# Gated linear attention and an MLP on one core: the gates' row-to-column transfers issued from ScalarE's queue

## The chip, the cores and the metric

The kernel runs on one core of a Trainium2 chip. The metric is the device time of one execution in microseconds (us). A core has five engines that run their own instruction streams: TensorE (PE), VectorE (DVE), ScalarE (ACT), GpSimd (POOL) and SyncE (SP). Transfers between the main memory and the on-chip memory are issued from the instruction stream of an engine; in this kernel all but two are issued from SP. Each stream is in order: an instruction that waits holds up everything behind it on its engine.

## The reference

The four attention inputs are float32. The weights of the MLP come as float64 and are rounded to float32 in the kernel.

```python
# q, k, v, alpha: (B, H, S, D) = (4, 8, 768, 48); alpha in 0.8 .. 1.0
for t in range(S):
    state = alpha[:, :, t, :, None] * state + einsum('bhd,bhe->bhde', k[:, :, t], v[:, :, t])
    y[:, :, t] = einsum('bhd,bhde->bhe', q[:, :, t], state)
x = y.transpose(0, 2, 1, 3).reshape(B, S, H * D)          # (4, 768, 384)
xn = (x - mean(x)) / sqrt(var(x) + 1e-6) * g_ln
out = x + maximum(xn @ w_ch1, 0) @ w_ch2                  # 384 -> 1536 -> 384
```

## The kernel before

The sequence of 768 steps is cut into 6 chunks of 128 rows, and with 4 batches this makes 24 attentions, called `a` to `x` (chunk `n // 4`, batch `n % 4`). Each handles all 8 heads of one batch and one chunk, as 4 pairs. In the chunks after the first, a chunk is treated as two halves of 64 rows.

One attention goes through these steps. ACT takes the logarithm of alpha (`la`, line 278); PE sums it along the rows with a triangular matrix (`lps`, 288); ACT takes the exponential of the sum and of its negative (`eq` and `lps`, 291 and 292); DVE multiplies k and q with them (`qk`, 294 and 296). The last row of `eq` in each half is the *gate*, by which the state is multiplied at the half's end. It lies along a row of one partition, and is wanted as a column, one value for each partition. This is done by two small transfers through main memory: SP writes the row to a buffer `row` (line 301), and later it reads it back as columns of 4-byte elements into `gate` (line 361). In between, PE transposes q and k (`tps`, 321), ACT (in the first chunk also DVE) copies them (`qT`, `kT`, 326 and 328), PE multiplies them (`aps`, 345; 337 in the first chunk) and DVE takes the part below the diagonal into `at` (350, 355). After the gate's transfer PE makes the halves' contributions to the state (`ups`, 371); DVE adds them to the old state and POOL multiplies with the gate (lines 384 and 386; in the first chunk one DVE instruction, 380). The result after the first half is `mid`, after the second the next state `st`. PE makes the output (`yps`, 407; 397 in the first chunk), which reads `mid`. Then come the norm on ACT (414 to 440; the first chunk's line 436 is on DVE), a copy of x to main memory (`kept`, 426), a transpose on PE (`xps`, 446) and a scaled copy (`xT`, 449 or 453).

The MLP of chunk 0 is plain (lines 476 and 488). For the other chunks both products are made with schemes of fewer block products (FIRST with 15 and SECOND with 20), whose sums are made on DVE, ACT and POOL (lines 575, 598 to 604, 739, 765 and on). The weights (`ws`, 192) are rounded in the first 95 us.

The order of all this is written out in the string ORDER: each letter is a turn of one generator (lower case: one attention; `M`, `V`, `N`, `X`, `R`, `S`, `W`, `O`, `Y`, `Z`, `P`, `Q`: parts of the MLP; `A` to `L`: one piece of the weights), which runs to its next `yield` and issues the instructions of one step. So ORDER fixes the order of the instructions on every engine. The waits are put in by the framework. The buffers `row` and `gate` exist four times each. All transfers, whichever engine issues them, take one of eight semaphores in turn, and a transfer waits until the one eight before it has landed.

The gate's step is a turn of its own, with nothing else in it, so that its place among the instructions of any engine can be read from ORDER.

Of the kernel before, what the change touches and what calls it, by code (L numbers as in the profile page):

```python
# [49 lines left out]
def kernel(  # L50
# [36 lines left out]
    nc = tc.nc  # L87
# [6 lines left out]
    NP = H // 2  # L94
# [18 lines left out]
    r = np.arange(P)  # L113
# [151 lines left out]
    def attention(c, b):  # L265
# [32 lines left out]
        ne = 1 if whole else 2  # L298
        row = dram.tile([2, 2 * 64 * NP], FP32, name="row", tag="row")
        gate = work.tile([P, 2, NP], FP32, name="gate", tag="gate", bufs=B)  # L300
# [57 lines left out]
                mask=mask_of_halves.unsqueeze(1).broadcast_to([P, 2 * NP, HS]))  # L358
        yield
        with nc.allow_non_contiguous_dma(reason="two rows to columns"):  # L360
            nc.sync.dma_start(gate[:, :ne], row[:ne].rearrange("o (p r) -> r o p", p=NP))
        yield
        vn, vx = raws["v", c, b]
        heads = [slice(0, 64), slice(64, R)]
# [475 lines left out]
    turns = {"YZ"[h]: first_of_chunk_0(h) for h in range(2)}  # L840
    turns |= {"PQ"[h]: second_of_chunk_0(h) for h in range(2)}
    turns |= {chr(ord("a") + n): attention(n // B, n % B) for n in range(NCB * B)}
    turns |= {chr(ord("A") + i): take_weights(i) for i in range(len(pieces))}
    turns |= {"M": mlp(), "V": hidden_products(NCB - 1), "S": combine_first(), "W": combine_weights(), "R": relus(),
# [34 lines left out]
```

## Time and profile before

| | |
|---|---|
| time, median of 3 runs | 445.36 us (441.68 to 449.35) |
| time of the profiled execution | 447.59 us |
| its span, first to last instruction | 445.8 us |
| mean granted TensorE clock | 0.988 |
| PE busy | 430.2 us (97%) |
| PE weight load busy | 385.2 us (86%) |
| DVE busy | 336.4 us (75%) |
| ACT busy | 202.2 us (45%) |
| POOL busy | 149.1 us (33%) |
| transfers | 45.53 MB in 54973 packets, 26204 of them under 512 B |
| issues of line 361 (gate) | 24, all from SP, between 12.6 and 279.0 us |

The busy time of an engine does not count the issuing of transfers and the waiting for semaphores. In the profile's lines an engine's name with a q (SPq, ACTq) means its instruction stream in such a step. The profiled execution is one execution, and its own time is above the median of the runs.

### The profile page before, as it was taken

The page shows a single profiled execution, that of the slowest core. Times are in us where ns is not written, and L with a number is a line of the kernel's source. Part 1 is how long each engine was busy: PE and PEld are TensorE (multiplying, and loading weights), DVE is VectorE, ACT ScalarE, POOL GpSimd, SP SyncE. Part 2 cuts the span into 40 slices and gives each one's busy share as a digit, 9 for nine tenths or more (in the row PEclk, how much of TensorE's full clock was granted, in tenths as well). Part 3 has the DMA queues.
Part 4 walks back from the last instruction along what each step waited for, and adds up shares of the span by engine and source line. Part 5 has one row for each costly group of instructions (what it writes and reads, how often), then busy time and mean ns, then how long its engine had stood idle before and what let it go on. Part 6 is the DMA issues. An engine that isn't in the chain of part 4 may idle for free.

```text
span 445.8 us, 11607 instructions
## 1 busy us (share of the span) xinstructions
PE 430.2 (97%) x4760; PEld 385.2 (86%) x4760; DVE 336.4 (75%) x654; ACT 202.2 (45%) x499; POOL 149.1 (33%) x164
## 2 busy tenths in 40 slices
PE   7987999999999999999999999997999999999996
PEld 5876988865778889998889998887999899999996
DVE  3895899989898788857679748665587689847873
ACT  6674746742422755653656156263223962014200
POOL 1021021200106472133763241680024680646523
PEclk9997999999999999999999999999899999999999
DMA  8889577782041425424341025200023000010201
GB/s 272 268 239 307 174 208 252 227 283 61 30 92 18 127 73 165 107 73 156 95 90 42 31 74 126 53 1 4 1 90 124 1 1 2 0 52 20 71 19 54
DMA packets 54973, 45.53 MB, mean 102 GB/s; under 512 B 26204, under 2 KB 51036, under 8 KB 54920
## 3 DMA queue, kind: packets, MB, share of 16 engines
q1 hardware_dynamic: 54376, 44.63, 34.2%
q8 instruction: 37, 0.61, 0.6%
q10 hardware_dynamic: 544, 0.17, 0.2%
q14 instruction: 16, 0.13, 0.1%
HBM read 35.25 MB, written 9.53 MB: 100 GB/s over the span
## 4 chain that ended last, share of the span: by engine, by line
PE 84%; DMA 5%; DVE 4%; issue 3%; SPq 2%; POOL 1%; ACT 1%; POOLq 0%; DVEq 0%
PE hps L765 29%; PE ops L588 25%; PE hps L476 7%; PE ops L488 7%; PE yps L407 4%; PE aps L345 3%; PE tps L321 3%; PE ups L371 2%; DMA ra<-in_alpha_dram 2%; PE xps L446 2%; DMA vn<-in_v_dram 2%; PE lps L288 1%; DMA ws<-in_moe_w_ch_dram 1%; POOL ob L604 1%; DMA ob<-kept 1%
## 5 line engine op out<-in xcount | busy, mean ns | idle before, releaser
L604 POOL TENSOR_TENSOR ob<-ob,u 128x192 f32<-128x192 f32 x40 | 25.2, 640 | 79.7 <-DVE ob L601 59.8
L765 PE MATMUL hps<-sum,w 128*128 128x256 f32 x192 | 47.3, 379 | 0.0
L588 PE MATMUL ops<-w,hT 128*128 128x192 f32 x224 | 41.0, 333 | 0.0
L765 PEld LDWEIGHTS hps<-sum,w 128*128 128x128 f32 x192 | 36.2, 190 | 4.8
L588 PEld LDWEIGHTS ops<-w,hT 128*128 128x128 f32 x224 | 38.2, 196 | 0.4
L816 ACT ACTIVATE hT<-hT 128x512 f32<-128x512 f32 x48 | 27.8, 626 | 19.2 <-POOL hT L787 11.9
L765 PE MATMUL hps<-xT,w 128*128 128x256 f32 x136 | 34.7, 380 | 0.0
L476 PE MATMUL hps<-xT,w 128*128 128x256 f32 x144 | 34.2, 391 | 0.1
L488 PE MATMUL ops<-w,hT 128*128 128x384 f32 x96 | 31.8, 486 | 0.0
L386 POOL TENSOR_TENSOR st<-st,gate 112x192 f32<-112x192 f32 x16 | 11.5, 726 | 60.4 <-DVE st L384 60.4
L476 PEld LDWEIGHTS hps<-xT,w 128*128 128x128 f32 x144 | 27.8, 198 | 4.3 <-issue 0.3
L386 POOL TENSOR_TENSOR mid<-mid,gate 112x192 f32<-112x192 f32 x20 | 12.3, 617 | 50.8 <-DVE mid L384 28.8
L598 DVE TENSOR_TENSOR ob<-ops,ob 128x192 f32<-128x192 f32 x50 | 17.1, 352 | 15.7 <-POOL ob L604 8.1
L588 PE MATMUL ops<-ws,sum 128*128 128x192 f32 x160 | 28.6, 326 | 0.0
L765 PEld LDWEIGHTS hps<-xT,w 128*128 128x128 f32 x136 | 25.4, 190 | 3.2
L488 PEld LDWEIGHTS ops<-w,hT 128*128 128x128 f32 x96 | 18.0, 190 | 11.5 <-issue 0.2
L588 PEld LDWEIGHTS ops<-ws,sum 128*128 128x128 f32 x160 | 26.4, 190 | 0.2
L407 PE MATMUL yps<-mid,qT 48*64 48x48 f32 x320 | 23.1, 224 | 3.0 <-issue 3.0
L321 PE MATMUL tps<-consts,qk 128*112 128x128 f32 x176 | 24.2, 275 | 1.2 <-DVE qk L296 1.1
L407 PE MATMUL yps<-vn,at 64*64 64x48 f32 x320 | 22.0, 225 | 1.8 <-issue 1.8
L407 PE MATMUL yps<-st,qT 48*64 48x48 f32 x320 | 23.7, 224 | 0.0
L345 PE MATMUL aps<-qT,kT 48*64 48x64 f32 x640 | 23.7, 222 | 0.0
(230 smaller groups left out, 1170.6 us busy)
## 6 DMA issues: line engine op xcount, KB each, us to landing
ws<-in_moe_w_ch_dram SPq DMA_DIRECT2D x12, 768.0 KB
vn<-in_v_dram SPq DMA_DIRECT2D x12, 384.0 KB
kept<-x SPq DMA_DIRECT2D x24, 192.0 KB
ob<-kept SPq DMA_DIRECT2D x24, 192.0 KB
out_dram<-ob SPq DMA_DIRECT2D x19, 192.0 KB
ra<-in_alpha_dram SPq DMA_DIRECT2D x16, 192.0 KB
rk<-in_k_dram SPq DMA_DIRECT2D x6, 384.0 KB
rq<-in_q_dram SPq DMA_DIRECT2D x6, 384.0 KB
```

The costliest lines, as they stand in the source:

```text
L321: nc.tensor.transpose(tps[:, p], qk_of(c, b)[:, i, p].rearrange("p a b -> p (a b)")[:, :R], ident)
L345: nc.tensor.matmul(aps[0][halves[1 - i], p, s], kT[rs, p, s], qT[rs, p, s], start=True, stop=True)
L371: nc.tensor.matmul(up[h, p], qk_of(c, b)[ts, 1, p, i, :h.stop - h.start], vn[ts, i, p], start=True, stop=True)
L386: nc.gpsimd.tensor_mul(new, new, by)
L407: nc.tensor.matmul(yps[r][halves[s], i, p], of, by, start=True, stop=True)
L476: nc.tensor.matmul(hps, w1[:, j // 2, f, j % 2 * P:][:, :P], xT_of[0][:, f, bs], start=(f == 0), stop=(f == NF - 1))
L488: nc.tensor.matmul(ops_of[b], hT_of[c][:, j, b], w2[:, j], start=(j == 0), stop=(j == NJ - 1))
L588: nc.tensor.matmul(acc, lhs[:, j], rhs[:, j], start=(j == 0), stop=(j == NT - 1))
L598: nc.vector.tensor_add(x, acc, x)
L604: getattr(nc.gpsimd, f"tensor_{op}")(x, x, y)
L765: nc.tensor.matmul(acc[:, i], w, b, start=True, stop=True)
L816: nc.scalar.activation(out=x, in_=x, func=AFT.Relu)
```

## The change

One line differs: the gate's second transfer, from `row` back into columns, is issued from ScalarE's instruction stream in place of SyncE's. ORDER stays as it is, so the issue stands between the ACT instructions of the turns around it. The first transfer, of the row to main memory, stays on SP, as do all others.

```diff
@@ -358,7 +358,7 @@
                 mask=mask_of_halves.unsqueeze(1).broadcast_to([P, 2 * NP, HS]))
         yield
         with nc.allow_non_contiguous_dma(reason="two rows to columns"):
-            nc.sync.dma_start(gate[:, :ne], row[:ne].rearrange("o (p r) -> r o p", p=NP))
+            nc.scalar.dma_start(gate[:, :ne], row[:ne].rearrange("o (p r) -> r o p", p=NP))
         yield
         vn, vx = raws["v", c, b]
         heads = [slice(0, 64), slice(64, R)]
```

## The prediction

> **What bounds the kernel now.** I read the page from the top: busy shares, the chain that ended last, then who waited for whom, then the two queues that the change touches.
>
> ```profile
> PE 430.2 (97%) x4760; PEld 385.2 (86%) x4760; DVE 336.4 (75%) x654; ACT 202.2 (45%) x499; POOL 149.1 (33%) x164
> ...
> PE 84%; DMA 5%; DVE 4%; issue 3%; SPq 2%; POOL 1%; ACT 1%; POOLq 0%; DVEq 0%
> ```
>
> TensorE is busy for 430.2 of 445.8 us and is 84% of the chain; ScalarE is 45% busy and 1% of the chain, SyncE's queue 2%. A change that touches only ACT and SP can win at most the 15.6 us in which PE is idle, and loses only what reaches PE. Where PE's idle time lies is told by its own waits:
>
> ```profile
> PE yps L407 <- issue: 4.8, 4, 1.8
> PE ups L371 <- issue: 2.3, 1, 2.3
> PE lps L284 <- ACT la L278: 1.4, 1, 1.4
> PE tps L321 <- DVE qk L296: 1.1, 3, 0.5
> ```
>
> The large ones (7.1 us) have no releaser that the profile shows; none names a gate. The tile view of the gate gives the price of what is moved, and who waits for it:
>
> ```profile
> L361 SPq DMA_DIRECT2D gate<-row x24: 355/392/733, 12.6 to 279.0; - x24
> ...
>   DMA gate<-row: 7.5, 2
> ```
>
> Twenty-four issues of 392 ns (median) on SP; only POOL waits for their landing, twice, 7.5 us together (gates f and h). SP itself waited little for the rows before it could issue them:
>
> ```profile
> SPq L361 <- DMA row<-eq: 2.0, 2, 1.2
> ```
>
> **Part 1: what leaves SP.** 24 x 0.392 = 9.4 us of issue, plus 2.0 us of waiting for rows, 11.4 us in all. The queue is seldom what ends a wait. The biggest ACT wait for a load (7.8 us, before the `la` of attention o at 110.75 us) stands behind an SP load that waits for VectorE, with no gate in between. The one place where gates stand before something early is 12.64 to 13.64 us, gates a and b ahead of row d and the weights' transfer at 14.04; these would come about 1 us sooner. VectorE takes those weights only at 21.23 us, in its own order, and was not idle for them. I take 0; the bound is a gain of 1 us there, and of 2 us more in the first 62 us, where the DMA engines are 79 to 87% busy and the 10 gates free 10 x 0.39 = 3.9 us of the queue (half of it, since SP waits for ACT, VectorE or PE between bursts).
>
> **Part 2: what ACT must do.** At its place in the order of turns ACT now issues the transfer. The nearest price is ACT's own two issues at the start:
>
> ```profile
> 0.76 0.38 ACTq L163 DMA_DIRECT2D consts<-consts  x1
> 1.17 0.52 ACTq L176 DMA_DIRECT2D small<-in_moe_g_ln_dram  x1
> ```
>
> The second has elements of 4 bytes too; the mean is 0.45 us, and 24 x 0.45 = 10.8 us, which takes ACT from 202 to 213 us. New waits on ACT: the row's landing, the gate buffer's last reader (four attentions back), and the transfer eight issues back, with which it shares its semaphore. I set the time at which ACT reaches each gate's place (end of the ACT instruction of the turn before) beside SP's issue: a 12.6 to 14.8, d 21.7 to 24.7, f 29.7 to 32.9, l 78.4 to 84.3, k 96.0 to 101.7, p 152.4 to 156.6, t 227.4 to 231.9, x 275.8 to 298.0, w 279.0 to 306.0; the others move by -1.1 (j) to +4 us. Except for j and h, about 1 us earlier, ACT comes no earlier than SP did, so what SP had waited for is there: I take 0 for waiting. For j and h the rows landed at 42 and 43 us, far ahead. The reverse wait (an SP transfer eight issues later, or a row four later, needs the gate landed) is also met: after gates x and w SP's eighth issue is at 327 and 332 us, while they land by 301 and 309.
>
> So the cost is 0.45 us in front of whatever ACT does next. At c, i, m, n, o, p, q, v and w ACT then idles 0.7 to 2.8 us anyway, waiting for PE as a rule: 9 gates hidden. At a and b (0.9 us together, before the qT copy at 14.72) the copy is used 5.7 us after it ends, and the `la` behind it 1.6 us after: hidden. For e, f, g, j, h, l, k, r, t, s, u and x I compared the ends of the next `la`, qT/kT and xn with PE's first matmul that takes them: 0.5 to 20 us of slack, hidden if no two delays add up. Gate d is not covered:
>
> ```profile
> 24.71 0.19 ACT L429 ACTIVATE few<-few 128x1 f32<-128x1 f32 x1
> ...
> 26.00 0.20 ACT L433 ACTIVATE few<-few 128x1 f32<-128x1 f32 x1
> ...
> 25.75 1.75 DVE L436 TENSOR_SCALAR xn<-x,few 128x384 f32<-128x384 f32 x2
> ```
>
> The second L436 starts at 26.23 us, as L433 ends, and is on the chain. I take **+0.45 us** for d. Uncovered, all 24 would cost 10.8.
>
> **Part 3: when the gate lands.** An idle-time SP gate lands 2.4 to 3.1 us after its issue (x: 275.78 to 278.13, by its semaphore); f, behind three loads of 384 KB, took 7.3. On ACT's queue the nearest row is `small`: its last 4-byte packet started at 4.36 us, 3.2 after the issue, while SP's load of 2.11 us needed until 7.35. So a separate queue passes loads that were issued earlier, and I take 3.2 us in the busy first 62 us and 2.6 later. The users:
>
> - a: 14.8 + 3.2 = 18.0, VectorE's `st` moves from 17.20 to 18.0 and ends at 18.35. Below, VectorE idles 0.93 us until 18.49: 0. With 4.0 us (SP's own a) it ends at 19.15: +0.7.
> - f: 32.9 + 3.2 = 36.1, 1 us before POOL got it (37.10). PE's next `yps` stalls until 40.86 for a reason the profile doesn't name: 0 either way, since even 7.3 us gives 40.2 + 0.5 = 40.7.
> - r: 195.5 + 2.6 = 198.1, against 199.06: VectorE's wait of 2.4 us behind it shrinks by up to 1 us; at 4.1 us of latency it grows by 0.6. I take 0; PE has four products of 1.3 us queued there.
> - w: 306.0 + 2.6 = 308.6 against POOL at 307.51: 1.1 late. Its `yps` is the third of three from 306.50 on and needs `mid` near 309.0; POOL now ends at 309.1: **+0.1 us**, with 3.2 us of latency +0.7. Behind it PE has a stall of 1.74 us (310.03) that could take it up.
>
> ```profile
> 17.20 0.35 DVE L380 TENSOR_TENSOR st<-ups,gate 112x192 f32<-112x192 f32 x1
> 18.49 0.55 DVE L294 TENSOR_TENSOR qk<-rk,lps 128x384 f32<-128x384 f32 x1 [0.93 <-ACT lps L292]
> ...
> 307.51 0.51 POOL L386 TENSOR_TENSOR mid<-mid,gate 112x192 f32<-112x192 f32 x1 [3.62 <-DVE mid L384]
> ```
>
> The others are used 2 us or more after they land, except l (84.3 + 3.2 = 87.5, POOL takes it at 88.35; with the 5.2 us it took on SP, 1.1 late).
>
> The row of `small` meets a rule that speaks against a gain: the Trainium skill, page "DMA: Bandwidth & Descriptors", section "Issuing engines are not separate DMA queues", says that transfers run on the same 16 engines whichever engine issues them and that another issuer saves only issue time. By the rule alone gate f would still need 7.3 us and gate a 4.0 us, the sum would be 1.3 us instead of 0.6; `small` speaks for a faster pass, and no run here shows it for a gate yet.
>
> **Sum.** 0.45 (d) + 0.1 (w) = +0.55 us on the profiled execution, 447.59 us (445.8 span, 1.8 around it): 448.1. That execution lies 2.2 us above the median of the runs (445.36), so the prediction is 445.36 + 0.55, rounded to **446.0 us**. Own range: -3 (part 1) to +0.45 + 0.7 + 0.6 + 0.7 + 1.1 = +3.6 us, 442.4 to 449.0, and the runs of before scatter by 4 us on each side.
>
> **Rivals.**
>
> 1. *ACT's issue reaches PE* (slower). The order of turns was laid out with no issue on ACT; if slack of 0.5 us is used up by an earlier delay, each gate costs PE its 0.45 us: 445.4 + 10.8 = 456.2. For: attentions e to v have `la`, qT/kT or xn with slack as small as 0.05 to 0.8 us (t's `la` 0.05, v's and x's xn 0.6). Against: none of these stands right behind a gate, and ACT idles often. It passes 2% when 20 of the 24 are exposed.
> 2. *SP's queue was holding the start* (faster). The 3 us of part 1 plus POOL's 2 us at f and h: 440.4. For: DMA 87% busy at the start. Against: PE waits there for ACT, VectorE or nothing named, not for a load. Even so it stays under 2%; to pass it, 8.9 of PE's 15.6 idle us must go.
> 3. *The gate doesn't land sooner on the other queue*, as the sixteen engines are shared: late landings at a, l, r, w cost 0.7 + 1.1 + 0.6 + 0.7 = 3.1, and d 0.45: 448.9, within 2%.
>
> Apart from these, PE's granted clock was 0.5 in three stretches of 3.4 us (about 1.7 us each); one more or less of them in a shifted start moves the time without any of my steps.
>
> **How the numbers follow.** The forecast (hidden but for half a microsecond) gets 0.55, rival 1 0.23, rival 2 0.10, rival 3 0.12. Two per cent, 8.9 us, is about what a measurement of this kernel can tell from no change. Slower by more: nearly all of rival 1 and a little of rival 3, 0.24. Faster by more: the best end of rival 2 with a clock stretch less, 0.06. Range: 441.0 (rival 2 nearly reached) to 456.0 (nearly all of rival 1); the forecast's own is 442.4 to 449.0.
>
> **What would show it.** Right: ACT busy unchanged but 24 ACTq issues of about 0.45 us, PE's waits still without a named ACT releaser, POOL's wait for gate f shorter than 4.3 us, gate w late by about 1 us. Wrong: ACT issues well above 0.5 us, waits of ACT on row or gate buffers, PE idle over 20 us with `kT`, `qT`, `xn` or `eq` as releasers; or PE idle under 8 us.

## The result: 1.0 % slower, and the profile after

| | before | after |
|---|---|---|
| median of 4 runs each | 444.17 us (441.68 to 449.35) | 449.08 us (448.63 to 451.27) |
| ratio of the times, 95% interval | | 1.0104 [1.0058, 1.0150] |
| profiled execution, its span | 447.59 us, 445.8 us | 448.63 us, 446.8 us |
| mean granted clock in it | 0.988 | 0.991 |
| PE's gaps between its first and last instruction, summed | 10.6 us | 12.4 us |

The change costs 4.9 us by the medians. That is within the 2 per cent that the prediction called no change, and yet the interval leaves no doubt of the sign. The forecast had +0.55 us. A ratio with an interval, here and below, leaves out the runs that took over 1.5% longer than the fastest run of their kernel on their chip; medians, means and the table of the clock take every run. The two profiled executions differ by 1.0 us only, because the one of before lay high for its kernel (447.59 against a median of 444.17), so one pair of traces can't hold the whole answer. That is why the same kernels ran again in the experiments below.

The page of the changed kernel, its busy shares, its two hardware queues and its chain:

```profile
PE 429.1 (96%) x4760; PEld 383.4 (86%) x4760; DVE 336.5 (75%) x654; ACT 202.5 (45%) x499; POOL 149.5 (33%) x164
...
q1 hardware_dynamic: 31464, 44.54, 31.1%
q10 hardware_dynamic: 23456, 0.26, 3.0%
...
PE 85%; DMA 6%; DVE 3%; issue 2%; SPq 1%; POOL 1%; ACT 1%; POOLq 0%; DVEq 0%
```

The work of each engine is the same to 2 us. Some 22,900 packets, nearly all of 4 bytes, have gone from SP's queue (q1) to ACT's (q10), which had 544 packets before. DMA has 6% of the chain in place of 5%.

The tile view of the gate (the same view as before the change: duration of one issue in ns, then first and last issue, who waited for its landing, and the time from issue to landing):

```profile
L361 ACTq DMA_DIRECT2D gate<-row x24: 366/367/465, 14.9 to 307.8; - x24
...
  POOL mid L386: 20.3, 4
  DVE st L380: 1.8, 1
...
DMA to landing us min/median/max: 2.5/2.5/4.4
```

An issue on ACT takes 367 ns, a little under the 0.45 us of the prediction. But POOL, which had waited twice for a gate, 7.5 us together, now waits four times, 20.3 us, and VectorE once, which it had not done. The last row has a trap. "DMA to landing" goes by few transfers here; the single landings, read from the releases in the timeline and the chain, run up to 9.2 us.

The waits of PE, POOL and SP (line waited at, releaser: us in total, times, longest):

```profile
PE yps L407 <- issue: 4.3, 3, 1.8
PE ups L371 <- issue: 2.3, 1, 2.3
...
PE ops L588 <- DVE st L384: 0.4, 1, 0.4
PE yps L407 <- POOL mid L386: 0.4, 1, 0.4
```

```profile
SPq L128 <- DMA gate<-row: 4.1, 1, 4.1
```

The two rows without a named releaser are there as before (6.6 us against 7.1), and three more such rows are new, 2.1 us together (`hps` L476 1.1, `hps` L765 0.7, `yps` L397 0.3). New are also two short waits whose releasers, `st` of VectorE and `mid` of POOL, stand just behind a gate (the one for `mid` is in the control below too, without the change), and three waits of SP for gates that ACT issued: the one shown and two at line 301, 3.2 us together.

The chain, in order of time (start, us, what), shows the two gates that are on it:

```profile
32.99 6.77 DMA gate<-row
...
196.65 4.26 DMA gate<-row
```

Gate f took 6.8 us from its issue at 32.99 us; gate r took 4.3 us in the quiet middle.

**Where the time went, along the span.** I matched the instructions of PE in the two traces one by one and took the difference of their starts, after less before. It is 0.57 us already at 12 us, before the first moved transfer, which is scatter. Then it steps to 1.04 us at 22 us (behind gate a) and 1.47 us at 30 us (a stall of 0.28 us with no named releaser is part of it). Around f, from 36 to 46 us, it runs between 1.1 and 2.3 us, and it is 1.58 us from 50 to 60 us, so that f leaves only 0.1 us in this pair. It is 2.56 us after 61 us (a stall of 1.12 us with no named releaser) and back at 1.44 us at 90 us. It stays at 1.59 us from 100 to 200 us, where seven gates are issued (r is the last). Gate r adds 0.40 us at 202 us, the `hps` stall behind it 0.3 us, gate w 0.1 us at 309 us. From 312 to 316 us the difference falls from 2.38 to 0.75 us. This last step is no gain of the change, as the windows of both traces show (from:to, length, busy time with the number of instructions of PE, of PE's weight load, of DVE, ACT and POOL, then PE's granted clock, the share of the DMA engines and GB/s). First before:

```profile
308.60:312.00 3.40, 1.66 (x111) 1.53 (x101) 3.07 (x6) 2.04 (x6) 0.00 (x0) 1.00 0.02 5
312.00:315.40 3.40, 3.40 (x22) 3.31 (x15) 0.00 (x0) 0.87 (x2) 0.00 (x0) 0.50 0.02 5
```

and after:

```profile
309.50:312.90 3.40, 2.10 (x129) 1.95 (x127) 1.82 (x5) 2.12 (x6) 0.51 (x1) 1.00 0.05 7
312.90:316.30 3.40, 2.17 (x25) 2.11 (x26) 1.46 (x3) 1.05 (x3) 0.00 (x0) 1.00 0.02 5
```

Before, PE had a stretch of 3.4 us at half clock here, which cost it some 1.7 us, half of its length; after had none. So in this pair after was lucky by 1.7 us, and its real cost is larger than the 1.0 us between the profiles.

### The profile page after: what moved, and what is told of

Its sections match the earlier page's. It is cut to its first block, busy times and chain, and to the rows that moved or that the text cites. A ratio compares the mean times of both kernels' runs of the same rounds, so it can differ in the third digit from the quotient of the medians.

```text
span 446.8 us, 11604 instructions
## 1 busy us (share of the span) xinstructions
PE 429.1 (96%) x4760; PEld 383.4 (86%) x4760; DVE 336.5 (75%) x654; ACT 202.5 (45%) x499; POOL 149.5 (33%) x164
## 4 chain that ended last, share of the span: by engine, by line
PE 85%; DMA 6%; DVE 3%; issue 2%; SPq 1%; POOL 1%; ACT 1%; POOLq 0%; DVEq 0%
PE hps L765 29%; PE ops L588 26%; PE ops L488 7%; PE hps L476 7%; PE yps L407 4%; PE tps L321 4%; PE aps L345 3%; DMA gate<-row 2%; PE ups L371 2%; DMA ra<-in_alpha_dram 2%; PE xps L446 2%; DMA rq<-in_q_dram 1%; PE lps L288 1%; DVE at L350 1%; POOL ob L604 1%
## 5 line engine op out<-in xcount | busy, mean ns | idle before, releaser
L765 PE MATMUL hps<-sum,w 128*128 128x256 f32 x192 | 47.3, 379 | 0.0
L765 PEld LDWEIGHTS hps<-sum,w 128*128 128x128 f32 x192 | 36.2, 190 | 4.8
L588 PE MATMUL ops<-w,hT 128*128 128x192 f32 x224 | 39.9, 327 | 0.0
L588 PEld LDWEIGHTS ops<-w,hT 128*128 128x128 f32 x224 | 36.8, 190 | 0.5
L765 PE MATMUL hps<-xT,w 128*128 128x256 f32 x136 | 34.7, 380 | 0.0
L476 PE MATMUL hps<-xT,w 128*128 128x256 f32 x144 | 33.6, 386 | 1.1 <-issue 1.1
L476 PEld LDWEIGHTS hps<-xT,w 128*128 128x128 f32 x144 | 27.4, 195 | 5.1 <-issue 1.3
L765 PEld LDWEIGHTS hps<-xT,w 128*128 128x128 f32 x136 | 25.4, 190 | 3.2
L488 PEld LDWEIGHTS ops<-w,hT 128*128 128x128 f32 x96 | 17.9, 190 | 11.7 <-DVE w L214 0.5
L407 PE MATMUL yps<-vx,at 64*64 64x48 f32 x320 | 22.2, 224 | 2.5 <-issue 2.5
```

Of the source, the lines that this page charges most:

```text
L407: nc.tensor.matmul(yps[r][halves[s], i, p], of, by, start=True, stop=True)
L476: nc.tensor.matmul(hps, w1[:, j // 2, f, j % 2 * P:][:, :P], xT_of[0][:, f, bs], start=(f == 0), stop=(f == NF - 1))
L488: nc.tensor.matmul(ops_of[b], hT_of[c][:, j, b], w2[:, j], start=(j == 0), stop=(j == NJ - 1))
L588: nc.tensor.matmul(acc, lhs[:, j], rhs[:, j], start=(j == 0), stop=(j == NT - 1))
L765: nc.tensor.matmul(acc[:, i], w, b, start=True, stop=True)
```

## The experiments

Two theories stood at the start. **Theory 1, late landings:** a gate on ACT's queue is issued later and lands no sooner, and where its user has little slack (a, f, g, r, w) the delay reaches PE. **Theory 2, ACT's issue:** each of the 24 issues delays ACT's next instruction, and part of that reaches PE. Letters are attentions in order, so that the kernels choose the engine by the letter. Each ratio is that of the kernel's runs to the runs of the kernel before on the same chip.

### Before and after once more

The kernel before, unchanged:

> The kernel before, unchanged, timed against itself. All theories expect 444 us and a ratio of 1.000; its profile shows how far two profiles of one program lie apart. In the profile of after PE's instructions run 0.57 us late from 8 us on, before the first moved transfer is issued at 14.9 us: if that is scatter, this profile scatters as much, and the half-clock stretches (three of 3.4 us before, two after) vary too.

Measured: 444.73 us, ratio 1.0027 [0.9989, 1.0065]. The method tells about 0.4% apart. One of PE's waits in its trace matters below:

```profile
PE yps L407 <- POOL mid L386: 0.3, 1, 0.3
```

This is the wait behind gate f, here with f on SP, and a stall of 1.9 us without a releaser stands behind it, as in the changed kernel.

After, again:

```diff
-            nc.sync.dma_start(gate[:, :ne], row[:ne].rearrange("o (p r) -> r o p", p=NP))
+            nc.scalar.dma_start(gate[:, :ne], row[:ne].rearrange("o (p r) -> r o p", p=NP))
```

> The changed kernel again, on the same chip as the three others. All theories expect 449 us and a ratio of 1.006 to 1.015; a ratio below 1.005 would say that most of the 4.6 us was the chip's scatter, and that the 1.8 us by which PE's instructions are late in the profile are the loss.

Measured: 449.08 us, ratio 1.0129 [1.0081, 1.0177]. The loss is real.

### Five gates moved, and the nineteen others

```diff
+            eng = nc.scalar if "abcdefghijklmnopqrstuvwx"[c * B + b] in "afgrw" else nc.sync
+            eng.dma_start(gate[:, :ne], row[:ne].rearrange("o (p r) -> r o p", p=NP))
```

> Only gates a, f, g, r and w are issued by ACT, the other 19 stay on SP. Theory 1: all of the loss, in the profile PE 1.8 us late at 310 us against the profile of before, by a 0.6, f and g 0.4, r 0.7, w 0.1; about 446 to 448 us. Theory 2: 5/24 of the loss, 445.0 us. Theory 3: f and g alone, SP again held about 4 us by gate g, 445 to 446 us.

Measured: 447.89 us, ratio 1.0107 [1.0061, 1.0153]. Five of the 24 gates cost about as much as all. In its trace PE is 1.2 us later from a on and waits 0.7 us behind r; f landed 6.2 us after its issue, and PE did not wait for it.

```diff
+            eng = nc.sync if "abcdefghijklmnopqrstuvwx"[c * B + b] in "afgrw" else nc.scalar
+            eng.dma_start(gate[:, :ne], row[:ne].rearrange("o (p r) -> r o p", p=NP))
```

> Gates a, f, g, r and w, whose readers waited for the landing in the profile of after, stay on SP; the other 19 are issued by ACT. Theory 1 (the loss is late landing): 0 to 0.5 us over before, about 444.5 us, ratio 1.000. Theory 2 (each issue of 0.37 us on ACT reaches PE): 19/24 of the loss of 4.6 us, 447.8 us, ratio 1.008. Theory 3 (4-byte packets on a queue of their own disturb the loads, and SP waits for gates that have not landed): i and the later ones do this too, but not where loads are dense; 445 us.

Measured: 447.06 us, ratio 1.0071 [1.0031, 1.0110]. This is more than theory 1 allows. The two halves add up to 1.78%, against 1.04 and 1.29% for the whole; measured against the control, which stands at 1.0027 itself, it is 1.24 against 1.02%, and that is no difference within the method's 0.4%. In its trace, PE's distance to the control is 3.0 us at 100 us, 3.4 us at 300 us and 3.1 us at the end, although twelve gates are issued from ACT after 84 us; so nearly all that it lost, it lost early. Of this, 0.9 us stand before the first moved gate (15.3 us), and the largest step, 1.9 us, stands at a stall of 4.3 us without a releaser, up to 43.3 us. The nineteen were then taken in two parts.

### The nineteen in two parts

```diff
+            eng = nc.scalar if "abcdefghijklmnopqrstuvwx"[c * B + b] in "lkmnopqtsuvx" else nc.sync
+            eng.dma_start(gate[:, :ne], row[:ne].rearrange("o (p r) -> r o p", p=NP))
```

> Only gates k to x without r and w (k, l, m, n, o, p, q, s, t, u, v, x; twelve, all issued after 84 us) are issued by ACT. Theory 1 (late landing): none of these has a reader that waited, so ratio 1.000, and PE's instructions keep their distance to the control from 100 us on to within 0.4 us. Theory 2 (each issue on ACT costs PE its 0.37 us): 12 x 0.37 = 4.4 us, ratio 1.010.

Measured: 445.03 us, ratio 1.0016 [0.9979, 1.0052].

Twelve issues of 366 ns on ACT, from 81 to 295 us, cost nothing that this ratio can tell. Theory 2 falls in its full size: at full exposure these twelve would have cost 12 x 0.37 = 4.4 us, 1.0%, and the interval ends at 0.5%. That the issues delay nothing on ACT is shown by its timeline, under part 2 below.

```diff
+            eng = nc.scalar if "abcdefghijklmnopqrstuvwx"[c * B + b] in "bcdejhi" else nc.sync
+            eng.dma_start(gate[:, :ne], row[:ne].rearrange("o (p r) -> r o p", p=NP))
```

> Only gates b, c, d, e, h, i and j, all issued in the first 60 us, are issued by ACT. Theory 1: i can land late (5.6 us in the profile of after), the others are not waited for: ratio 1.000 to 1.003. Theory 2: 7 x 0.37 = 2.6 us, ratio 1.006. Rival of dense loads (any 4-byte packets on their own queue in this stretch cost, read or not): ratio 1.004 to 1.008.

Measured: 446.05 us, ratio 1.0037 [0.9995, 1.0079]. This decides nothing. If the early seven cost something, it is under 0.8%.

### Which of the five

```diff
+            eng = nc.scalar if "abcdefghijklmnopqrstuvwx"[c * B + b] in "fg" else nc.sync
+            eng.dma_start(gate[:, :ne], row[:ne].rearrange("o (p r) -> r o p", p=NP))
```

> Only gates f and g are issued by ACT. Theory 1 (late landing is the loss, with a and r as its places): f and g land late but in a stretch where PE waits anyway, so 0 to 0.5 us; with the time lost to half clock taken out, about 441.8 us against 441.6 before. Rival (the 4-byte packets on a queue of their own among dense loads are the loss: f took 5.9 us and g 9.2 us to land, and SP stood 4 us behind g): the whole 2.7 us of the five gates, 444.3 us. The profile should show the packets of f and g spread over 4 to 5.5 us on the ACT queue.

Measured: 447.20 us, ratio 1.0051 [1.0021, 1.0082], more than I expected. POOL and PE in its trace (the bracket gives the idle time before and its releaser):

```profile
41.06 0.51 POOL L387 TENSOR_TENSOR mid<-mid,gate 112x192 f32<-112x192 f32 x1 [8.90 <-DMA gate<-row]
```

```profile
PE yps L408 <- POOL mid L387: 2.5, 1, 2.5
```

Gate f, issued at 30.98 us, landed 9.9 us later, and PE waited 2.5 us for the `mid` made of it. In the second run of after this wait was 2.1 us, in the first 0.4 us, and with five gates moved there was none. It is not a loss of its own, though: where the wait is long, the stall without a releaser that stands at this place in the other traces is missing. Both together are 1.4 to 2.5 us in the four traces with f on ACT, and 1.6 to 4.3 us in the six with f at its place on SP (1.8 before, 2.2 in the control). So no trace shows what f and g cost, and the 0.5% stands without a cause.

```diff
+            eng = nc.scalar if "abcdefghijklmnopqrstuvwx"[c * B + b] in "ar" else nc.sync
+            eng.dma_start(gate[:, :ne], row[:ne].rearrange("o (p r) -> r o p", p=NP))
```

> Only gates a and r are issued by ACT. Theory 1: PE's instructions are late by 0.5 to 1.3 us from 20 us on (a, through VectorE's st) and by another 0.5 to 0.7 us from 201 us on (r, PE waits for VectorE's st); with half clock taken out 443 to 443.5 us against 441.6. Rival (dense loads, f and g): 441.6 us.

Measured: 446.01 us, ratio 1.0000 [0.9962, 1.0037]. VectorE in its trace:

```profile
19.44 0.36 DVE L381 TENSOR_TENSOR st<-ups,gate 112x192 f32<-112x192 f32 x1 [2.27 <-DMA gate<-row]
```

Gate a landed 5.45 us after its issue and VectorE waited 2.3 us for it; behind gate r PE waited 0.6 us for `st`. Matched to the control, PE is about 1 us later from a on and 0.6 to 0.9 us from r on. The time does not show these 1.6 us; its interval allows 0.37%, which is as much. So for a and r there is a wait in every trace where they were moved, and no loss that this ratio confirms. By the means of all twelve runs and of all 35 of the kernel before, the ratio is 1.0028, and with the clock taken out (below) the two cost 2.0 us (+-0.9).

### Issued earlier, on either queue

If lateness is the fault, a gate issued earlier should not lose, on whichever queue. In the chunks after the first the transfer can stand behind the qT copy of the same attention, some turns earlier. Gates a to d keep their place and SP.

```diff
+                if not whole:
+                    with nc.allow_non_contiguous_dma(reason="two rows to columns"):
+                        nc.scalar.dma_start(gate, row.rearrange("o (p r) -> r o p", p=NP))
...
-        with nc.allow_non_contiguous_dma(reason="two rows to columns"):
-            nc.sync.dma_start(gate[:, :ne], row[:ne].rearrange("o (p r) -> r o p", p=NP))
+        if whole:
+            with nc.allow_non_contiguous_dma(reason="two rows to columns"):
+                nc.sync.dma_start(gate[:, :ne], row[:ne].rearrange("o (p r) -> r o p", p=NP))
```

> Gates a to d stay on SP; the other 20 are issued by ACT, but earlier, right after the qT copy of the same attention (r about 8 us earlier than in the changed kernel). Theory 1: no loss, ratio 0.995 to 1.003; POOL's mid of r and w no longer wait for a landing. Theory 2 (each issue on ACT costs): 20/24 of the loss as before, ratio 1.008. Rival of dense loads: f and g still travel among loads, ratio 1.004 to 1.006.

Measured: 447.24 us, ratio 1.0029 [0.9999, 1.0058]. By this ratio it loses less than after does (the intervals of this and of the second run of after don't meet), but it is not shown to lose nothing: by the means of all runs it is 1.0069, against 1.0102 for the second run of after. It scatters most of all (443.69 to 453.87 us), and its mean clock, 0.990 over 12 runs, is as low as after's. In its trace a new wait stands on ACT, which issues the gate behind the copy and so waits for the row:

```profile
50.45 0.59 ACT L328 COPY qT<-tps 112x512 f32<-112x512 f32 x1 [3.99 <-DMA row<-eq]
```

PE then waited 3.9 us for the `la` behind it (53.2 us), and two half-clock stretches followed (52.7 to 59.5 us). So this version has a loss that late landings don't explain, and it is no clean test of theory 1.

The same place, on SP:

```diff
+                        nc.sync.dma_start(gate, row.rearrange("o (p r) -> r o p", p=NP))
```

> As the last one, but the early issue is on SP, so ACT is as before. Theory 1: not slower than before, ratio 0.990 to 1.000, since r's 2.4 us wait on VectorE in the kernel before goes; theory 2 the same. If SP, which now waits for rows that have just been sent, holds back its loads, up to 1.01.

Measured: 442.90 us, ratio 0.9948 [0.9913, 0.9983], the only version that beats both kernels. Once more:

> The kernel with the early issue on SP once more, to see whether its gain holds: ratio 0.990 to 0.999, about 442.5 us, with less time at half clock than the kernel before (1.6 us against 2.8).

Measured: 442.78 us, ratio 0.9977 [0.9939, 1.0016], an interval that holds 1. Together, 24 runs have a median of 442.8 us, against 444.8 us for the 98 runs of the kernel before: a gain of about 0.4%, shown by the first run and not by the second alone. By the table below, the gain goes with the clock. VectorE and PE in its first trace:

```profile
195.27 0.36 DVE L388 TENSOR_TENSOR st<-ups,mid 112x192 f32<-112x192 f32 x1 [0.62 <-POOL mid L390]
```

```profile
PE yps L411 <- POOL mid L390: 1.6, 1, 1.6
```

At gate r, VectorE's wait is 0.62 us (2.36 us before, 2.76 us after), and POOL has no wait for a gate in this trace (in the second one, a single wait of 3.6 us). PE's gaps add up to 7.0 us, against 10.6 before and 12.4 after.

### The clock, over all runs

Each run has a granted clock. Of the 98 runs of the kernel before, the 9 with a clock of 0.998 or more have a median of 441.1 us, the 37 around 0.996 have 443.5, the 43 around 0.991 have 445.9, and the 9 below 0.9895 have 447.6. A straight line through all runs of all kernels, with one height for each kernel, gives 1.10 us (+-0.14) of time for each microsecond of clock lost, where the loss is (1 - clock) x 445 us. Its heights and losses split the difference:

| | runs | mean, us | clock lost, us | time less 1.10 x loss |
|---|---|---|---|---|
| before | 98 | 444.7 | 2.9 | 441.5 +-0.5 |
| after | 10 | 449.2 | 4.5 | 444.2 +-1.1 |
| five moved | 6 | 447.9 | 3.4 | 444.2 +-1.3 |
| nineteen moved | 12 | 446.7 | 3.5 | 442.8 +-1.0 |
| f, g moved | 12 | 447.1 | 4.2 | 442.5 +-1.0 |
| a, r moved | 12 | 446.0 | 2.2 | 443.6 +-0.9 |
| twelve late moved | 12 | 445.5 | 2.6 | 442.6 +-0.9 |
| seven early moved | 12 | 445.6 | 3.2 | 442.1 +-0.9 |
| earlier, on ACT | 12 | 447.8 | 4.5 | 442.9 +-1.0 |
| earlier, on SP | 24 | 443.0 | 1.3 | 441.2 and 441.9 |

Of after's 4.5 us, 1.10 x 1.6 = 1.8 us go with the clock and 2.7 us (+-1.0) do not. The same 2.7 us (+-1.2) come from the five gates alone, in its parts 2.0 us from a and r and 1.0 us from f and g (+-0.9 each). The twelve late gates stand 1.1 us (+-0.9) above before, which their ratio did not show. The gain of the early issue on SP is all clock: its losses are 1.6 us smaller, and its height is that of before. A straight line shows that the two go together, and not which causes which; the windows below show the order in time.

## Why the prediction was right and wrong

**The forecast and its sum.** The direction, the class and the middle of the span were right: PE's distance is flat from 100 to 200 us, the sum is small, and 449.08 lies just above the forecast's own range (442.4 to 449.0). The sum itself, +0.55 us, was too small by a factor of 8 to 9, and of its two terms the large one, +0.45 us for gate d, measured nothing (part 2). The class was in part luck: rival 3 has the same class with other steps, and it is nearer to what happened.

**Part 1 (SP's queue).** Taken at 0. The traces show no gain there. That SP could gain by *order* was not seen: issued earlier on SP, the gates won 0.4%.

**Part 2 (ACT's issue).** Right that it costs next to nothing, wrong in its price and in one statement. An issue is 367 ns, not 450; ACT is busy for the same 202 us; no wait of ACT for a row or a buffer appeared; the twelve late gates cost 0.16% with zero well inside. But the price does not stand "in front of whatever ACT does next". Gate d, first before and then after:

```profile
23.91 0.49 ACT L291 ACTIVATE more<-lps 128x384 f32<-128x384 f32 x1 [1.06 <-PE lps L288]
```

```profile
24.95 0.49 ACT L291 ACTIVATE more<-lps 128x384 f32<-128x384 f32 x1 [1.25 <-PE lps L288]
25.02 0.37 ACTq L361 DMA_DIRECT2D gate<-row  x1
...
25.75 0.19 ACT L429 ACTIVATE few<-few 128x1 f32<-128x1 f32 x1
```

The issue (25.02 to 25.39 us) runs while L291 is still busy. From L291 to L429 it is 0.80 us, and it was 0.80 us before (23.91 to 24.71): the term of +0.45 us measured 0.00. For 21 of the 24 gates the time between the ACT instructions on both sides of the issue is not more than 0.08 us longer than before. Only a and b, issued one behind the other, put off the qT copy by 0.6 us, and l its next instruction by 0.2 us. The rows from which the price was taken show the same: both issues (0.76 to 1.69 us) lie inside ACT's table load (0.73 to 2.01 us).

The statement that failed is "the reverse wait is also met". It was worked out for the end, behind gates x and w, and not for g:

```profile
41.50 0.37 SPq L128 DMA_DIRECT2D rk<-in_k_dram  x1
46.06 0.37 SPq L128 DMA_DIRECT2D rq<-in_q_dram  x1
```

These are two of SP's issues in the changed kernel, one after the other. SP reached the second at 41.9 us and stood for 4.1 us, since gate g, issued by ACT eight transfers earlier, had not landed until 45.99 us. This `rq` went out 4.7 us later than in the trace of before (41.37 us). PE's distance does not grow between 46 and 60 us, so no price of this shows.

**Part 3 (when the gate lands) is the step that failed**, and in it the number 3.2 us. It came from `small`, which went out when four loads of SP were just starting. The landings that were then measured:

| gate | on SP, before | forecast on ACT | on ACT, measured | effect on PE |
|---|---|---|---|---|
| a | 4.0 us | 3.2, effect 0 | 4.6 to 5.5 | +0.5 to +1.3 us |
| f | 7.3 | 3.2, "0 either way" | 6.2 to 9.9 | none beyond the scatter |
| g | 5.4 | 3.2, 0 | 4.4 to 9.2 | with f |
| r | 4.0 | 2.6, 0 | 4.3 to 4.5 | +0.4 to +0.7 us |
| w | 2.5 | 2.6, +0.1 | 2.4 | +0.1 us |

In the quiet stretches the estimate was right (x 2.15 us, w 2.4 us). Under loads a gate on ACT's queue takes about as long as one on SP's, at times longer, and g was shorter in two of four traces (4.4 and 4.6 us). The timelines of the changed kernel show a and f, with ACT's issue and the user behind it:

```profile
14.86 0.52 ACT L278 ACTIVATE la<-ra 128x384 f32<-128x384 f32 x1 [2.46 <-DMA ra<-in_alpha_dram]
14.93 0.93 ACTq L361 DMA_DIRECT2D gate<-row  x2
```

```profile
19.64 0.36 DVE L380 TENSOR_TENSOR st<-ups,gate 112x192 f32<-112x192 f32 x1 [1.79 <-DMA gate<-row]
19.92 0.54 DVE L294 TENSOR_TENSOR qk<-rk,lps 128x384 f32<-128x384 f32 x1
```

```profile
39.90 0.51 POOL L386 TENSOR_TENSOR mid<-mid,gate 112x192 f32<-112x192 f32 x1 [5.90 <-DMA gate<-row]
```

ACT could not issue gate a before 14.93 us, behind the `la` that waited for a load (SP: 12.64 us). The landing at 19.5 us makes VectorE's `st` end at 20.0 us; the bound of the prediction, 19.15 us, had the 4.0 us of SP's gate for its worst case, and not more. Everything behind `st` on VectorE is `qk`, which PE's transposes wait for: `qk` moved from 18.49 to 19.92 us. For f, "even 7.3 us gives 40.7" had the landing right for this trace (39.76 us) and trusted that PE's unnamed stall until 40.86 us would still cover it. Here the stall stands *behind* the wait for `mid` (40.8 us, 1.75 us), but so it does in the control, with f on SP, and the two together are 2.2 us in both. In the two traces with the longest waits (2.1 and 2.5 us) the wait takes the stall's place. So the forecast's "0" for f holds within the scatter, while its landing was wrong by a factor of two to three.

For r, the timelines of POOL, VectorE and PE:

```profile
201.05 0.51 POOL L386 TENSOR_TENSOR mid<-mid,gate 112x192 f32<-112x192 f32 x1 [5.46 <-DMA gate<-row]
```

```profile
201.59 0.36 DVE L384 TENSOR_TENSOR st<-ups,mid 112x192 f32<-112x192 f32 x1 [2.76 <-POOL mid L386]
```

```profile
202.00 1.57 PE L588 MATMUL ops<-w,sum 128*128 128x192 f32 x8 [0.42 <-DVE st L384]
```

The working named this very case ("at 4.1 us of latency it grows by 0.6") and its cover, PE's queued products; the latency was 4.3 us, VectorE's wait grew by 0.4 us, and the cover lacked 0.42 us. The nearest row was the 4.0 us that the same gate had on SP; the quiet 2.6 us was the wrong choice. So what failed in part 3, by its effect on PE, is the landing at a and r: +0.5 to +1.3 and +0.4 to +0.7 us where the sum had 0.

**Rival 3** (the gate doesn't land sooner) is what happened, in its mechanism and, by its 448.9 us, nearly in its size; it had 0.12. Its size is partly chance: its 3.1 us of landings counted l (1.1 us), where no step appears, its 0.45 us for d measured nothing, and 1.8 us of the measured loss go with the clock. The forecast weighed the row of `small` against the Trainium skill's page "DMA: Bandwidth & Descriptors", section "Issuing engines are not separate DMA queues", and followed the row. The measurements of f and g (4.4 to 9.9 us beside loads, against 7.3 and 5.4 us on SP) agree with the page: no saving of transfer time by the other issuer shows in them.

**Rival 1** (ACT's issue reaches PE, 0.23) is refuted in its size by the twelve late gates, and in its mechanism by ACT's timeline at gate d. **Rival 2** (SP's queue was holding the start) has no sign in after.

**The clock** was an aside ("one more or less of them moves the time without any of my steps"). It should have been a term: what delays PE at one place by 1 to 2 us can bring a half-clock stretch of 1.7 us more, and in the mean the runs of after lost 1.8 us more with the clock than those of before.

**What stays open.** The early seven gates (1.0037 [0.9995, 1.0079]) and the loss of the nineteen that lies before 100 us; the 0.5% of f and g and the 1.1 us of the twelve late gates, for which no trace shows a wait. PE's stalls without a releaser (1.4 to 4.3 us near 33, 40 and 310 us) fall together with fetches of instructions by their times, but no run tested it.

## What to carry to other kernels

Price a transfer that moves to another queue by when the new engine *reaches* its place, behind whatever load it waits for, and by landings of the same kind of transfer under the load of that stretch; a quiet landing is a price only for quiet stretches. Don't add the issue's time to the new engine before a row shows that its instructions move apart. If a small transfer is late, try issuing it earlier where it is before looking for another queue. And where the matrix engine sets the end, count a new stall of 1 to 2 us twice: once for itself, and once for the clock that may drop after it.

## What the runs showed of the hardware

**The clock falls after a half-empty window, not only after an idle one.** In twelve of the thirteen profiles PE's clock fell to 0.5 within the span for stretches of 3.41 us (or twice that). On a grid of windows of 3.41 us laid through these stretches, each of the 20 windows at full clock in which PE was busy for up to 0.49 of the time was followed by a half-clock one; from 0.56 up none was; 0.53 and 0.54 were not, 0.55 once was. Windows that ran at half clock themselves don't all fit: three were followed by a second one, with PE busy 0.37, 0.85 and 0.96. Two examples, from the changed kernel and from its second run:

```profile
33.10:36.50 3.40, 1.14 (x56) 1.05 (x48) 1.49 (x5) 1.51 (x4) 0.51 (x1) 1.00 1.05 254
36.50:39.90 3.40, 3.40 (x89) 2.87 (x81) 2.68 (x6) 2.19 (x7) 0.00 (x1) 0.50 0.87 277
```

```profile
86.60:90.00 3.40, 1.88 (x71) 1.59 (x67) 2.52 (x5) 1.86 (x6) 3.06 (x3) 1.00 0.81 248
90.00:93.40 3.40, 3.40 (x10) 2.65 (x9) 2.98 (x6) 0.74 (x3) 0.00 (x0) 0.50 0.92 297
```

PE was busy 0.34 and 0.55 of the first window, and the second ran at half speed. A stall of about 1.7 us is enough if it falls into one window; the same stall across the border of two windows costs nothing more (309.5 to 316.3 us, shown above: 0.62 and 0.64). The Trainium skill, page "TensorE: Matmul & The Clock Gate", Part 1, has the half rate and the window of about 3.4 us, and both agree with these runs. The same page's advice to avoid idle gaps of more than about 3 us (section "Why this matters for your kernels") does not go far enough here, where gaps of 1.5 to 2.5 us brought the clock down.

**A small transfer on its own queue is still slow beside loads.** Gate f has 1040 packets of 4 bytes. In the changed kernel they took from 35.2 to 39.4 us, while the core's queues moved some 230 GB/s; gate x, alone, took 0.8 us for the same number (300.8 to 301.6 us).

**One sixteenth can come late.** Of gate r, 975 packets had landed by 198.90 us, and the other 65, the share of one DMA engine, came at 200.08 to 200.46 us, after a fetch of 16 KB of instructions at 198.3 us that took about 0.96 us. Gates i and m show the same, and so does r on SP before: fifteen of its sixteen shares had landed by 197.50 us, the last at 198.93 us, after a fetch at 196.7 us. That the fetch is the cause is read from these times, and was not tested.
